# Expert 1's first weights fetched into another tile, three clears of the output moved forward, and the first-layer copies put in another order, in a fused attention and mixture-of-experts kernel

## The chip, the cores and the metric

The kernel runs on one NeuronCore of a Trainium2 chip. The metric is the device time of one execution in microseconds (us). Three runs of the kernel before took 678.64, 680.66 and 685.27 us; the median is 680.66 us. One more execution was profiled; it took 679.25 us, of which 677.5 us lie between the first and the last instruction.

The engines are named as the profile names them: PE (TensorE, matrix multiply), PEld (its weight loads), DVE (VectorE), ACT (ScalarE), POOL (GpSimd) and SP (SyncE, which here only issues transfers). Each engine works through its own instructions in the order in which they were written. SP and POOL each issue transfers in that order too, so a transfer whose source isn't ready holds back every later transfer of the same issuer.

## The reference, cut to what matters

An attention layer over 4 batches, 8 heads, 768 positions and head size 64 feeds a mixture of 8 experts.

```
scores_l = q k^T / 8          kept where |i - j| < 16, else -1e9
scores_s = q kmax^T / 8 + log(32)   kmax: maximum of k over each block of 32
a   = softmax over [scores_l, scores_s]
x   = a [v ; mean of v over each block]          -> 3072 tokens x 512
noisy = x w_gate + log(1 + exp(x w_noise)) * noise
top2, weights = two largest of 8 per token, softmax over the two
out = 0
for e in 8 experts:
    h = relu(x[tokens of e] @ w1[e])      512 -> 1024
    out[tokens of e] += weight * (h @ w2[e])   1024 -> 512
```

All values are float32. The kernel writes every float32 factor of the two expert products as a float16 high part plus a float16 low part and multiplies high by high, high by low and low by high.

## The kernel before, in words

**Attention.** 24 tiles `t` of 128 tokens (128 rows of one batch) run through a software pipeline: in round `t` of the loop at L1087 the scores of tile `t + 2`, the transposes of the probabilities of tile `t + 1`, the product with v of tile `t` and the transpose of the finished x of tile `t - 1` are issued. `norm(t)` (L335) divides by the softmax sum and leaves `X[t]`. `norm_hi` and `norm_lo` (L347 to L358) split it into the high and the low half of `XR[t]`, a tile name with three buffers, so tile `t + 3` takes the buffer of tile `t`; `x_out` (L360) writes it to the DRAM table `xd`. What doesn't belong to the pipeline (the gate in batches of four tiles, loads of weights, transfers) is put at a place `at(time, function)` (L991), where the whole part is the round and the fraction the place in it; `run` issues it there. `.9` is close to the end of a round, ahead of the `x_out(t - 2)` that ends it. After the loop a written-out tail (L1141 to L1221) finishes the last tiles, the gate and the first half of expert 0's first layer; in it DVE carries the gate's small operations one after another.

**Gathers.** Each expert has 816 slots in seven chunks `c`, six of 128 and one of 48. `x_gather(e, c)` (POOL) fetches the x rows of the tokens of a chunk into one of four tiles `XG` (or, for expert 1's first three chunks, `PREV`), `x_trans(e, c)` (SP, a transposing transfer) turns them into `XTE[e]`; expert 0's last three chunks are transposed on PE instead (`x_trans_pe`, L770). Results are added to `out` in DRAM by a gather of the old rows, a DVE operation `y_out` (L954), and a scatter. So `out` must be zero first: `clear(zero, n)` (L996) writes n x 128 rows of zeros from a zeroed tile, 768 KB for n = 3. All eight clears are issued by SP in the tail, after `x_out(23)`.

**Weights.** `w_load(e, i)` (L617) brings one 512 KB block into one of four buffers of the tile `stg`: blocks 0 to 3 are w1 (128 rows each), 4 to 7 are w2. Before a buffer is loaded again, the operations that read it must be over. `w_hi` and `w_lo` make the halves for w2.

**First layer, expert 0** (`mm1`): twelve matmuls for each of the eight column blocks f of w1. **First layer, experts 1 to 7** (`mm1_all`, L836): Winograd's form of the 2 x 2 block product, with seven products instead of eight. It needs sums of blocks of w1 (`w1_sums` on DVE, L653, from blocks k and k + 2; `w1_hi` on ACT, L672; `w1_lo` on DVE, L676; the results for the sums lie in `sh` and `sl`, one pair for even and one for odd experts) and sums of quarters of x (`t_all`, `t_two`, `t_four` on DVE, or `t_diff` on POOL with `t_join` on DVE; `t_hi` on ACT, `t_lo` on DVE; L690 to L724). For each f of four, products 1 to 7 come in the order of `ROUNDS` (L834), a minus sign meaning the f of the round before; product 3 closes the PSUM tile `DD[f]`, and `after` (L842) issues what follows a product: copies of PSUM to SBUF on ACT (`P1`, `U2`, `U3`), additions on DVE (`A`, `DD`, `C22`), and `h_hi` (ACT) and `h_lo` (DVE), which make the halves of h. Product 4 of f adds into the PSUM tile from which `U3[f]` is copied, so it waits for that copy.

**Second layer** (`mm2_turn`, L969): three passes of eight matmuls for a chunk, then `y_out`. The PSUM tile `pt` has two buffers, so the chunk after next waits for `y_out`.

**Order across experts.** Between products and passes a tick is counted, and a plan (L1251 to L1310) tells what each tick issues: `steps(n, e, ...)` puts steps for expert n into the ticks of expert e. In expert 0, ticks 0 to 2 follow the last passes of chunks 0 to 2, ticks 3 to 10 the eight blocks f of the second half of its first layer, and three ticks each follow the passes of chunks 3 to 6. In the others ticks 0 to 27 follow the 28 products. `d` (L1297) shifts the `t_diff` and `t_join` steps that are issued during expert 1.

Of the kernel before, what the change touches and what calls it, by code (L numbers as in the profile page):

```python
# [8 lines left out]
F32 = mybir.dt.float32  # L9
# [11 lines left out]
P = 128  # L21
# [39 lines left out]
def attn_moe(ctx, tc, qt, kt, vt, wgn, noise, w1, w2, out):  # L61
# [552 lines left out]

    SG = {}

    def w_load(e, i):  # L617
        s = stage.tile([P, SW], F32, name="stg")[:, :1024]
        SG[e, i] = s
        if i < 4:  # L620
            nc.sync.dma_start(s, w1[e, i * P:(i + 1) * P, :])
        else:
            i -= 4
            nc.sync.dma_start(s.rearrange("p (c d) -> p c d", c=2),
                              w2[e, 2 * i * P:2 * (i + 1) * P, :].rearrange("(c p) d -> p c d", p=P))
# [202 lines left out]
    def h_hi(f, c0, c1, c):  # L828
        nc.scalar.activation(HT[0][:, f, c0:c1], c, AF.Relu)  # L829

    def h_lo(f, c0, c1, c):
        nc.vector.scalar_tensor_tensor(HT[1][:, f, c0:c1], c, 0.0, HT[0][:, f, c0:c1], op0=OP.max, op1=OP.subtract)
# [3 lines left out]
    def mm1_all(e, tick):  # L836
        X, DD, A, P1, U2, U3, C22 = {}, {}, {}, {}, {}, {}, {}

        def temp(name, n=1):
            return side_pool[0].tile([P, HC], F32, name=name, bufs=n)  # L840

        def after(f, p):  # L842
            g = f + FC // 2
            if p == 1:
                P1[f] = temp("p1")
                nc.scalar.activation(P1[f], X[f], AF.Copy)  # L846
                if f:
                    h_hi(g - 1, HC, CAP, C22[f - 1])
            elif p == 2:
                nc.vector.tensor_add(A[f], A[f], P1[f])  # L850
                if f:
                    h_lo(g - 1, HC, CAP, C22[f - 1]) if f < 3 else None
                h_hi(f, 0, HC, A[f])
            elif p == 4:
                h_hi(g, 0, HC, X[f])
            elif p == 6:
                U2[f] = temp("u2", 2)
                nc.scalar.activation(U2[f], X[f], AF.Copy)
            elif p == 3:
                nc.vector.tensor_add(DD[f], DD[f], U2[f])  # L860
                h_hi(f, HC, CAP, DD[f])
            elif p == 7:
                U3[f] = temp("u3")
                nc.scalar.activation(U3[f], X[f], AF.Copy)
                C22[f] = temp("c22")
                nc.vector.tensor_add(C22[f], DD[f], U3[f])

        for r, ps in enumerate(ROUNDS):
            for p in ps:
                f = r - (p < 0)  # L870
                p = abs(p)
                if p == 1:
                    X[f] = bank()[:, 0, :HC]
                elif p == 5:
                    DD[f] = bank()[:, 0, :HC]
                elif p == 2:
                    A[f] = accs[0].tile([P, 512], F32, name="a")[:, :HC]
                o = DD[f] if p in (3, 5) else A[f] if p == 2 else X[f]
                product(o, e, f, p, p in (1, 5, 2), p in (4, 3, 2))
                after(f, p)  # L880
                g = FC // 2
                if r < 3:
                    if p == 6:
                        h_lo(f, 0, HC, A[f])
                        if f:
                            h_lo(f - 1 + g, 0, HC, X[f - 1])
                    elif p == 3:
                        pass
                    elif p == 7 and f:
                        h_lo(f - 1, HC, CAP, DD[f - 1])  # L890
                else:
                    if p == 6:
                        h_lo(2 + g, HC, CAP, C22[2])
                        h_lo(2 + g, 0, HC, X[2])
                    elif p == 4 and f == 3:
                        h_lo(2, HC, CAP, DD[2])
                    elif p == 2:
                        h_hi(3 + g, HC, CAP, C22[3])
                        h_lo(3 + g, 0, HC, X[3])
                    elif p == 3 and f == 3:  # L900
                        h_lo(3, 0, HC, A[3])
                        h_lo(3 + g, HC, CAP, C22[3])
                        h_lo(3, HC, CAP, DD[3])
                tick()
# [86 lines left out]
    def at(t, f, *a):  # L991
        todo.setdefault(round(t, 3), []).append((f, a))
# [50 lines left out]
    for i in range(3):  # L1043
        at(4.9 + 2 * i, fill, i)
    at(20.8, last_init)
    for b, (t0, t1) in enumerate(BATCH[:4]):
        u = t1 + 2
        at(u - 0.91, gate_gt, b)
        at(u - 0.91, gate_gc, b)
        at(u + 0.09, gate_gl, b)  # L1050
        at(u + 0.09, gate_gd, b)
        at(u + 0.9, gate_a, b)
        at(u + 1.1, gate_b, b)
        at(u + 1.1, gate_m, b)
        at(u + 1.9, gate_p, b)
        at(u + 2.3, lambda b, t: gate_c(b, PO[t]), b, u + 2)
        at(u + 3.02, lambda b, t: gate_d(b, PO[t]), b, u + 2)
        at(u + 3.1, gate_e, b)
        if b == 3:
            break  # L1060
        at(u + 4.1, gate_v, b)
        z = u + (6 if b < 2 else 4)
        at(z + 0.2, gate_o, b)
        at(z + 0.2, gate_f, b, (0,))
        at(z + 1.03, gate_f, b, (1,))
        at(z + 1.9, lambda b, t: gate_t(b, PO[t]), b, z + 1)
        at(z + 2.02, lambda b, t: gate_u(b, PO[t]), b, z + 1)
# [113 lines left out]
    norm_hi(NT - 1)  # L1181
    norm_lo(NT - 1, nc.vector)
    x_out(NT - 1)
    for i in range(8):
        clear(PREV[2], 3)
    for x in HT:
        nc.gpsimd.memset(x[:, :, CAP:], 0.0)
# [35 lines left out]
    def finish_table():  # L1223
        decode(TB.rearrange("p e c w -> p (e c) w"), 0, NS)
        last_ids()
        for c in range(3, NCH):
            x_gather(0, c)
        for f in range(4, 8):
            w_lo(0, f)
        for c in range(3):  # L1230
            x_gather(1, c)
        w_load(1, 0)
        x_trans(0, 3)
        w_load(1, 2)
        x_trans(1, 0)
        x_trans(1, 1)
        w_load(1, 1)
        x_trans(1, 2)
        w_load(1, 3)

    finish_table()
    mm2_high(0, 0)
# [21 lines left out]
    for k, c in ((0, 3), (1, 4), (1, 5), (2, 6)):  # L1264
        put(0, k, x_gather, 1, c)
        put(0, k, x_trans, 1, c)
    steps(1, 0, (
        (2, w1_hi, 0, 0), (3, w1_sums, 0, 0), (3, w1_sums, 0, 1), (3, w1_hi, 0, 1), (4, w1_lo, 0, 0),
        (5, w1_lo, 0, 1, (0,)), (6, w1_lo, 0, 1, (1,)), (6, w1_sums, 1, 0), (6, w1_hi, 1, 0), (7, w1_sums, 1, 1),
        (7, w1_hi, 1, 1), (8, w1_lo, 1, 0), (9, w1_lo, 1, 1, (0,)), (10, w1_lo, 1, 1, (1,)), (10, t_all, 3),  # L1270
        (11, t_alloc), (11, t_two, 0), (11, t_two, 1), (11, t_hi, 3), (11, t_hi, 2), (13, t_all, 1), (13, t_hi, 1),
        (14, t_lo, 3), (14, t_lo, 2), (16, t_lo, 1), (16, t_four), (16, t_hi, 4), (19, t_lo, 4)))
    for i, k in enumerate((14, 16, 18, 19)):
        put(0, k, w_load, 1, 4 + i)
    M2 = 7 * (FC // 2)
# [10 lines left out]
    for e in range(1, E):  # L1286
# [7 lines left out]
            break  # L1294
        n = e + 1
        put(e, 0, w1_alloc, n, True)
        d = 6 if e == 1 else 0  # L1297
        steps(n, e, (
            (1 + d, t_diff, 3, 0), (4 + d, t_diff, 3, 1), (10 + d, t_join, 3),
            (7 + d, t_diff, 1, 0), (11 + d, t_diff, 1, 1), (17 + d, t_join, 1)))  # L1300
# [149 lines left out]
```

## Time and profile before

| | us |
|---|---|
| three runs | 678.64, 680.66, 685.27 |
| profiled execution, its own time | 679.25 |
| its span, first to last instruction | 677.5 |
| PE busy | 639.6 (94%) |
| DVE busy | 492.7 (73%) |
| ACT busy | 318.6 (47%) |
| POOL busy | 319.3 (47%) |
| granted clock of TensorE | 0.994 |
| bytes moved | 125.64 MB |

The attention takes the first 140 us or so, the tail and expert 0 run until about 222 us, and each of the other seven experts takes a little over 63 us. A row of a timeline tells the start, the duration, the engine, the line, the operation, what it writes and reads, and in square brackets how long its engine was idle before and which instruction ended that. In the windows, the columns are the stretch, its length, the busy time and the number of instructions of each engine, the granted clock, the share of the 16 DMA engines that was busy, and GB/s. Ends of matmuls are modelled: a matmul row reaches a little beyond the place where the next one may start.

### The profile page before, as it was taken

The page shows a single profiled execution, that of the slowest core. Times are in us where ns is not written, and L with a number is a line of the kernel's source. Part 1 is how long each engine was busy: PE and PEld are TensorE (multiplying, and loading weights), DVE is VectorE, ACT ScalarE, POOL GpSimd, SP SyncE. Part 2 cuts the span into 40 slices and gives each one's busy share as a digit, 9 for nine tenths or more (in the row PEclk, how much of TensorE's full clock was granted, in tenths as well). Part 3 has the DMA queues.
Part 4 walks back from the last instruction along what each step waited for, and adds up shares of the span by engine and source line. Part 5 has one row for each costly group of instructions (what it writes and reads, how often), then busy time and mean ns, then how long its engine had stood idle before and what let it go on. Part 6 is the DMA issues. An engine that isn't in the chain of part 4 may idle for free.

```text
span 677.5 us, 14084 instructions
## 1 busy us (share of the span) xinstructions
PE 639.6 (94%) x5408; PEld 368.5 (54%) x5408; DVE 492.7 (73%) x905; ACT 318.6 (47%) x679; POOL 319.3 (47%) x459
## 2 busy tenths in 40 slices
PE   7999889989999999999999999999999999999992
PEld 6777667755444654555455445544654555455442
DVE  5748798999479788677958795788688687946410
ACT  2879788852251554156325523542463156326100
POOL 3454344430833656562856276545556551640141
PEclk9999999999999999999999999999999999999997
DMA  8999999769995956727554564567266622431120
GB/s 285 290 294 301 296 313 296 244 159 369 262 189 128 262 178 169 231 88 206 149 183 151 163 192 160 181 156 242 94 167 165 225 84 89 169 109 32 33 84 31
DMA packets 99241, 125.64 MB, mean 185 GB/s; under 512 B 57929, under 2 KB 62801, under 8 KB 99164
## 3 DMA queue, kind: packets, MB, share of 16 engines
q1 hardware_dynamic: 87020, 88.37, 45.8%
q0 software_dynamic: 12144, 36.28, 17.2%
q8 instruction: 44, 0.72, 0.5%
q14 instruction: 33, 0.27, 0.1%
HBM read 87.57 MB, written 26.21 MB: 168 GB/s over the span
## 4 chain that ended last, share of the span: by engine, by line
PE 70%; DVE 11%; ACT 7%; DMA 6%; issue 3%; POOL 1%; SPq 0%; POOLq 0%; DVEq 0%; ACTq 0%
PE pt L939 34%; PE h L824 21%; PE a L824 4%; PE pt L936 3%; DMA stg<-in_w_dram 2%; ACT p L310 2%; DMA hth<-in_vt_dram 1%; DMA q<-in_qt_dram 1%; PE h L788 1%; PE s L296 1%; PE pt L316 1%; DVE rh L541 1%; DVE t L649 1%; ACT pts L319 1%; ACT w2h L629 1%
## 5 line engine op out<-in xcount | busy, mean ns | idle before, releaser
L92 POOL DMA_INDIRECT out_dram<-y,tb x48 | 64.7, 1347 | 165.6 <-DVE y L962 152.3
L939 PEld LDWEIGHTS <-hth 128*128 128x128 f16 x768 | 74.7, 98 | 91.7 <-ACT hth L798 2.5
L939 PE MATMUL pt<-w2h,hth 128*128 128x512 f16 x376 | 89.0, 379 | 2.2 <-ACT hth L798 1.4
L92 POOL DMA_INDIRECT xg<-xd,tb x53 | 68.0, 1282 | 46.2 <-DVE oc L567 24.8
L939 PE MATMUL pt<-w2h,htl 128*128 128x512 f16 x376 | 89.0, 379 | 0.6 <-DVE htl L799 0.6
L939 PE MATMUL pt<-w2l,hth 128*128 128x512 f16 x376 | 88.8, 379 | 0.0
L824 PE MATMUL h<-tx,sh 128*128 128x408 f16 x336 | 78.7, 336 | 0.0
L962 DVE SCALAR_TENSOR_TENSOR y<-pt,tb,prev 128x512 f32<-128x512 f32 x42 | 31.5, 749 | 53.9 <-PE pt L939 53.9
L646 DVE SCALAR_TENSOR_TENSOR w2l<-stg,w2h 128x1024 f16<-128x1024 f32 x32 | 48.5, 1524 | 28.0 <-ACT w2h L629 28.0
L824 PEld LDWEIGHTS <-w1h 128*128 128x128 f16 x448 | 43.2, 98 | 36.6 <-issue 4.7
L939 PEld LDWEIGHTS <-htl 128*128 128x128 f16 x384 | 37.6, 98 | 46.3 <-DVE htl L799 1.1
L693 POOL TENSOR_TENSOR t<-xte 128x816 f32<-128x816 f16 x24 | 41.5, 1755 | 34.5 <-DVE t L649 29.9
L824 PE MATMUL h<-xte,w1h 128*128 128x408 f16 x224 | 57.0, 336 | 0.0
L92 POOL DMA_INDIRECT prev<-out_dram,tb x42 | 50.9, 1212 | 12.7 <-issue 12.7
L358 POOL TENSOR_TENSOR xr<-x,xr 128x512 f16<-128x512 f32 x22 | 25.4, 1156 | 62.8 <-PE pt L316 28.8
L310 ACT ACTIVATE p<-s,nm 128x118 f32<-128x118 f32 x192 | 53.4, 377 | 0.8
L721 ACT ACTIVATE tx<-t 128x816 f16<-128x816 f32 x28 | 24.0, 879 | 55.0 <-DVE t L649 55.0
L846 ACT ACTIVATE p<-h 128x408 f32<-128x408 f32 x28 | 14.3, 512 | 69.2 <-PE h L824 68.9
L824 PEld LDWEIGHTS <-sh 128*128 128x128 f16 x336 | 32.9, 98 | 25.2 <-issue 0.2
L829 ACT ACTIVATE hth<-h 128x408 f16<-128x408 f32 x56 | 27.7, 508 | 36.2 <-DVE h L860 35.0
L824 PE MATMUL h<-tx,sl 128*128 128x408 f16 x168 | 42.7, 336 | 0.0
L674 ACT ACTIVATE sh<-ws 128x1536 f16<-128x1536 f32 x14 | 20.8, 1483 | 41.0 <-DVE ws L649 33.0
(205 smaller groups left out, 1239.1 us busy)
## 6 DMA issues: line engine op xcount, KB each, us to landing
stg<-in_w_dram SPq DMA_DIRECT2D x64, 512.0 KB
hth<-in_vt_dram SPq DMA_DIRECT2D x8, 780.0 KB
vw<-in_vt_dram SPq DMA_DIRECT2D x32, 195.0 KB
q<-in_qt_dram SPq DMA_DIRECT2D x24, 256.0 KB
xd<-xr SPq DMA_DIRECT2D x24, 256.0 KB
out_dram<-prev SPq DMA_DIRECT2D x8, 768.0 KB
kb<-in_kt_dram SPq DMA_DIRECT2D x6, 768.0 KB
htl<-in_vt_dram SPq DMA_DIRECT2D x16, 195.0 KB
```

Source lines behind the costliest of these rows:

```text
L92: return nc.gpsimd.indirect_dma_start(**kw)
L310: nc.scalar.activation(PE_[t][:, a, hp, :], SC[t][:, a, hp, :], AF.Exp, bias=NM[t][:, 1, a, hp:hp + 1], scale=0.125)
L358: engine.tensor_tensor(XR[t][:, DM:], X[t], XR[t][:, 0:DM], op=OP.subtract)
L646: nc.vector.scalar_tensor_tensor(lo, SG[e, i], sc, hi, op0=OP.mult, op1=OP.subtract)
L674: nc.scalar.activation(h, x, AF.Copy, scale=W1S)
L693: nc.gpsimd.tensor_tensor(tt(e, 0 if low else j), xb(e, *i, low), xb(e, *o, low), op=OP.subtract)
L721: nc.scalar.activation(TX[e][:, 0, j - 1], t_of(e, j), AF.Copy)
L824: nc.tensor.matmul(o, lhs[a][:, c], rhs[b][:, c], start=start and n == 0, stop=stop and n == 5, skip_group_check=True)
L829: nc.scalar.activation(HT[0][:, f, c0:c1], c, AF.Relu)
L936: nc.tensor.matmul(py[64 * r:64 * r + 64, :HD], hx[:, f, c * P:c * P + 64], w[:, f, HD * r:HD * r + HD], start=first, stop=final, skip_gro ...
L939: nc.tensor.matmul(py, hx[:, f, c * P:c * P + P], w[:, f, :], start=first, stop=final, skip_group_check=True)
L962: nc.vector.scalar_tensor_tensor(y, py[:, :d], gw, pv[:, :d], op0=OP.mult, op1=OP.add)
```

## The change

Four edits stand in the diff.

- **Loads.** `w_load` can take another home than `stg`: a tile under the name `sh0` or `sl0`, which later holds the sums of expert 2's weights and has the room for a block. Blocks 0 and 2 of expert 1's w1 go there and are issued right after `x_out(23)`. Blocks 1 and 3 take the two earlier places in `finish_table`. The steps that work on expert 1's w1 move up by about two ticks, and `t_lo` of one quarter by one tick.
- **Clears.** Three of the eight clears are put into the attention, at 21.9, 22.8 and 22.9, with `XG[3]` (zeroed at the start) as their source; five stay after the two loads.
- **First-layer order.** For f = 0, 1 and 2, `h_hi(f)` of `DD[f]` isn't issued behind the DVE addition that follows product 3, but behind the copy `U3` of the next f (f = 0, 1), or behind product 4 of f = 3 (f = 2).
- **Sums of x.** `d` is 7 instead of 6: the `t_diff` and `t_join` steps during expert 1 come one tick later.

```diff
-    def w_load(e, i):
-        s = stage.tile([P, SW], F32, name="stg")[:, :1024]
+    def w_load(e, i, home=None):
+        if home:
+            s = late[0].tile([P, 3 * HF], F32, name=home)[:, :1024]
+        else:
+            s = stage.tile([P, SW], F32, name="stg")[:, :1024]
...
             elif p == 3:
                 nc.vector.tensor_add(DD[f], DD[f], U2[f])
-                h_hi(f, HC, CAP, DD[f])
+                if f == FC // 2 - 1:
+                    h_hi(f, HC, CAP, DD[f])
             elif p == 7:
                 U3[f] = temp("u3")
                 nc.scalar.activation(U3[f], X[f], AF.Copy)
+                if 0 < f < FC // 2 - 1:
+                    h_hi(f - 1, HC, CAP, DD[f - 1])
                 C22[f] = temp("c22")
...
                     elif p == 4 and f == 3:
+                        h_hi(2, HC, CAP, DD[2])
                         h_lo(2, HC, CAP, DD[2])
...
     at(20.8, last_init)
+    for t in (21.9, 22.8, 22.9):
+        at(t, lambda: clear(XG[3].bitcast(F32), 3))
...
     x_out(NT - 1)
-    for i in range(8):
+    w_load(1, 0, "sh0")
+    w_load(1, 2, "sl0")
+    for i in range(5):
         clear(PREV[2], 3)
...
         for c in range(3):
             x_gather(1, c)
-        w_load(1, 0)
+        w_load(1, 1)
         x_trans(0, 3)
-        w_load(1, 2)
-        x_trans(1, 0)
-        x_trans(1, 1)
-        w_load(1, 1)
-        x_trans(1, 2)
         w_load(1, 3)
+        for c in range(3):
+            x_trans(1, c)
...
     steps(1, 0, (
-        (2, w1_hi, 0, 0), (3, w1_sums, 0, 0), (3, w1_sums, 0, 1), (3, w1_hi, 0, 1), (4, w1_lo, 0, 0),
-        (5, w1_lo, 0, 1, (0,)), (6, w1_lo, 0, 1, (1,)), (6, w1_sums, 1, 0), (6, w1_hi, 1, 0), (7, w1_sums, 1, 1),
-        (7, w1_hi, 1, 1), (8, w1_lo, 1, 0), (9, w1_lo, 1, 1, (0,)), (10, w1_lo, 1, 1, (1,)), (10, t_all, 3),
-        (11, t_alloc), (11, t_two, 0), (11, t_two, 1), (11, t_hi, 3), (11, t_hi, 2), (13, t_all, 1), (13, t_hi, 1),
-        (14, t_lo, 3), (14, t_lo, 2), (16, t_lo, 1), (16, t_four), (16, t_hi, 4), (19, t_lo, 4)))
+        (0, w1_sums, 0, 0), (1, w1_sums, 0, 1), (2, w1_hi, 0, 0), (2, w1_hi, 0, 1), (2, w1_lo, 0, 0),
+        (3, w1_lo, 0, 1, (0,)), (4, w1_lo, 0, 1, (1,)), (4, w1_sums, 1, 0), (4, w1_hi, 1, 0), (5, w1_sums, 1, 1),
+        (6, w1_lo, 1, 0), (6, w1_hi, 1, 1), (7, w1_lo, 1, 1, (0,)), (8, w1_lo, 1, 1, (1,)), (10, t_all, 3),
+        (11, t_alloc), (11, t_two, 0), (11, t_hi, 3), (11, t_two, 1), (11, t_hi, 2), (13, t_all, 1), (13, t_hi, 1),
+        (13, t_lo, 3), (14, t_lo, 2), (16, t_lo, 1), (16, t_four), (16, t_hi, 4), (19, t_lo, 4)))
...
-        d = 6 if e == 1 else 0
+        d = 7 if e == 1 else 0
```

## The prediction

> **What bounds the kernel now.** I read the page first, then the windows of ten us, then the chain of work that ended last, and then the timelines of the engines where PE has gaps. From the page, and from the windows:
>
> ```profile
> span 677.5 us, 14084 instructions
> PE 639.6 (94%) x5408; PEld 368.5 (54%) x5408; DVE 492.7 (73%) x905; ACT 318.6 (47%) x679; POOL 319.3 (47%) x459
> ...
> 150.00:160.00 10.00, 8.02 (x61) 5.05 (x60) 9.76 (x29) 4.89 (x8) 0.00 (x0) 1.00 0.87 318
> 200.00:210.00 10.00, 8.01 (x37) 3.19 (x36) 8.17 (x11) 3.26 (x5) 4.12 (x6) 1.00 0.86 192
> 210.00:220.00 10.00, 9.06 (x49) 4.24 (x49) 9.83 (x12) 2.65 (x3) 5.14 (x7) 1.00 0.25 71
> ```
>
> PE is the bound, busy 94% of the span. Only its gaps can be won, and the windows tell two kinds: around 150 DVE is full (9.76 of 10) and PE waits for it; around 200 to 220 PE loses some 3 us again. The chain of waits names what lies behind the second, and gives the pace of the later experts:
>
> ```profile
> 142.99 2.56 DMA xd<-xr
> ...
> 185.03 12.27 DMA stg<-in_w_dram
> ...
> 222.29 1.14 PE h L824 x6
> ...
> 252.56 31.08 PE pt L939 x144
> 283.64 2.74 PE pt L936 x48
> 286.38 1.14 PE h L824 x6
> ...
> 293.73 6.21 PE h L824 x36
> ...
> 315.74 31.08 PE pt L939 x144
> ...
> 631.74 31.08 PE pt L939 x144
> ```
>
> In these rows (start, duration, what) a second layer takes 31.08 us for six chunks, 5.18 each, and 2.74 for the last. Thirty-six matmuls, six products, take 6.21, so a product takes 1.035; the first of an expert is 1.14. Twenty-eight products without a stall would be 1.14 + 27 x 1.035 = 29.08. Expert 1 takes 252.56 - 222.29 = 30.27, so it loses 1.19. Expert 2 takes 315.74 - 286.38 = 29.36 and loses 0.28. From 315.74 to 631.74 lie five experts at 63.20, less 33.82 for their second layers: 29.38, so experts 3 to 7 lose 0.28 to 0.30 as well.
>
> **Part one: expert 1's first weights.** The PE rows at the passage from expert 0 to 1, then the rows of DVE, ACT and SP that stand behind them:
>
> ```profile
> 200.34 0.81 PE L939 MATMUL pt<-w2h,hth 128*128 128x512 f16 x3
> 202.55 1.25 PE L939 MATMUL pt<-w2h,hth 128*128 128x512 f16 x5 [1.40 <-ACT hth L798]
> ...
> 213.98 1.89 PE L939 MATMUL pt<-w2h,hth 128*128 128x512 f16 x8 [0.78 <-DVE y L960]
> ```
>
> ```profile
> 179.81 0.75 DVE L960 TENSOR_SCALAR y<-pt,tb 128x512 f32<-128x512 f32 x1 [1.42 <-PE pt L939]
> ...
> 208.08 1.00 DVE L649 SCALAR_TENSOR_TENSOR t<-xte 128x816 f32<-128x816 f16 x1
> ...
> 213.18 0.75 DVE L960 TENSOR_SCALAR y<-pt,tb 128x512 f32<-128x512 f32 x1
> ```
>
> ```profile
> 197.33 1.06 ACT L674 ACTIVATE w1h<-stg 128x1024 f16<-128x1024 f32 x1 [4.50 <-DMA stg<-in_w_dram]
> ```
>
> ```profile
> 169.60 0.36 SPq L621 DMA_DIRECT2D stg<-in_w_dram  x1
> ...
> 173.32 0.51 SPq L621 DMA_DIRECT2D stg<-in_w_dram  x1
> ...
> 185.03 1.56 SPq L621 DMA_DIRECT2D stg<-in_w_dram  x1
> ```
>
> Chunk 3 starts at 200.34. Three chunks and the last one need 3 x 5.18 + 2.74 = 18.28, yet expert 1 starts at 222.29, 21.95 later. So 3.67 are lost, of which I count 3.6 (the chain begins a step a little later than the row does). It is a chain of lateness: the fourth w1 block is issued at 185.03 and lands 12.27 later, ACT has been idle 4.50 for it, `hth` comes late behind it on ACT (1.40), and DVE, which does the last w1 pieces until 208.08, then `t_all`, gets to `y` of chunk 3 only at 213.18, while PE waits for that PSUM buffer (0.78); two smaller gaps have the same origin.
>
> With the change blocks 0 and 2 need no `stg` buffer and are issued near 151; blocks 1 and 3 go out at 169.60 and 173.32. Even with the 12.27 of the slowest row the last lands by 185.6. It is wanted at tick 4, behind the second block f of the first layer, near 190: 4 us of cover. One window more, from 182 to 208 (the third busy time is DVE's):
>
> ```profile
> 182.00:208.00 26.00, 23.43 (x129) 11.76 (x128) 18.13 (x25) 11.11 (x17) 10.22 (x18) 1.00 1.01 205
> ```
>
> DVE had 18.13 us of work there and nearly 8 idle. The first sums move ahead of it: two ticks of two operations of 512 columns, 1.25 us a tick at the 1.00 that 816 columns take at 208.08, and DVE is idle for 1.42 before the `y` at 179.81. So about 15.6 remain from 182 on, without the wait, and DVE could be through near 198. It is then held by PE's own end of the first layer (200.34), with one ACT and one DVE operation behind it (0.5 to 0.6 each, as the rows of L829 and L860 below): `t_all` starts near 201.7 instead of at 208.08, 6.4 earlier. `y` of chunk 3 moves from 213.18 to 206.8; PE wants its buffer at 200.34 + 2 x 5.18 = 210.7. That is 3.9 of cover, and all four gaps go: **-3.6**. What is late next is nothing of DVE, but PE itself. The `t_lo` that moves a tick keeps its place behind `y` on DVE, and swapping `t_hi` with `t_two` crosses two engines: no cost, as both queues keep their order. The tile for the blocks belongs to expert 2's sums, which are first written in tick 33 of expert 1, in its second layer (after 252.56), some 50 us after the last reader. With two blocks fewer in `stg`, expert 1's first w2 blocks find a free buffer without waiting for w1.
>
> **Part two: the order in the first layer.** PE's row in expert 1 with DVE's; then ACT's two rows in expert 2:
>
> ```profile
> 244.12 0.51 PE L824 MATMUL h<-tx,w1h 128*128 128x408 f16 x2 [1.03 <-ACT u L864]
> ```
>
> ```profile
> 241.62 1.00 DVE L649 SCALAR_TENSOR_TENSOR t<-t,t 128x816 f32<-128x816 f32 x1
> 242.54 0.58 DVE L860 TENSOR_TENSOR h<-h,u 128x408 f32<-128x408 f32 x1
> ```
>
> ```profile
> 306.33 0.51 ACT L829 ACTIVATE hth<-h 128x408 f16<-128x408 f32 x1 [1.79 <-DVE h L860]
> 306.74 0.51 ACT L864 ACTIVATE u<-h 128x408 f32<-128x408 f32 x1
> ```
>
> PE waits for `U3` (L864). `U3` waits on ACT behind `h_hi` (L829), that for the DVE addition L860, and that, in expert 1, stands behind a `t_join` of 1.00 (L649). In experts 2 to 7 it stands behind a w2 operation. With `h_hi` behind `U3`, the copy starts when its product ends: ACT was idle 1.79 before. So ACT's 0.41 between the two starts and all of DVE's delay leave the path. Product 7 of f = 2 is the nineteenth and ends at 286.38 + 1.14 + 18 x 1.035 = 306.15, so `U3` is out near 306.75, and PE wants it one product after 306.15, at 307.19: cover 0.4. For expert 1 the later `t_join` (d = 7) cures the same stall a second time. `t_diff` on POOL comes a tick later, 1.035, with its `t_join` a tick later too, so POOL keeps its distance; no `y` scatter is behind it. `h_hi(2)` goes behind product 4 of f = 3 and swaps with `h_hi(7)`; both are done at the same time as before, and `h_lo(2)` about 0.8 later, ahead of the sum for `A[3]`, which the second layer reads as its seventh matmul, 1.3 after its start: cover 0.5, at a cost of zero to 0.3 per expert if it is gone. Sum: expert 1 **-1.2**, the six others 6 x 0.28 = **-1.7**.
>
> **Part three: the clears.** The end of the attention on SP, what follows on ACT, DVE and PE, and three windows of 2 us:
>
> ```profile
> 137.38 0.52 SPq L361 DMA_DIRECT2D xd<-xr  x1
> ...
> 142.99 8.02 SPq L361 DMA_DIRECT2D xd<-xr  x4
> 151.11 9.18 SPq L999 DMA_DIRECT2D out_dram<-prev  x8
> ```
>
> ```profile
> 149.32 0.61 ACT L351 ACTIVATE xr<-x 128x512 f16<-128x512 f32 x1
> ```
>
> ```profile
> 149.97 0.69 DVE L358 TENSOR_TENSOR xr<-x,xr 128x512 f16<-128x512 f32 x1 [0.16 <-ACT xr L351]
> ```
>
> ```profile
> 145.04 0.81 PE L788 MATMUL h<-xte,w1h 128*128 128x384 f16 x4
> ...
> 158.60 0.45 PE L551 MATMUL o<-rh,lh 128*128 128x168 f16 x4 [0.32 <-DVE rh L541]
> ```
>
> ```profile
> 142.00:144.00 2.00, 1.28 (x16) 0.66 (x18) 1.92 (x17) 1.31 (x4) 1.18 (x5) 1.00 0.82 135
> ...
> 148.00:150.00 2.00, 2.00 (x16) 1.23 (x15) 1.74 (x18) 0.79 (x3) 0.00 (x0) 1.00 0.04 9
> ...
> 152.00:154.00 2.00, 1.18 (x12) 0.97 (x12) 1.90 (x12) 0.96 (x2) 0.00 (x0) 1.00 1.00 378
> ```
>
> The first clear comes ahead of `x_out(19)` (137.38) and two transposes, the other two ahead of `x_out(20)` (142.99). Clears alone ran at 378 GB/s, so one of 0.786 MB takes 2.1 us and two take 4.2. `x_out(20)` took 2.56 to land; behind two clears it lands at 142.99 + 2.56 + 4.2 = 149.75. Its `XR` buffer is written next by `norm_hi(23)`, on ACT at 149.32: 0.43 late. Queued behind that are `norm_lo(23)` on DVE at 149.97, the full DVE stream after it, and PE, which waits for DVE at 158.60; so the delay reaches the end. The first clear delays the transposes that the matmuls read at 145.04; SP issued the last of them just ahead of its row at 142.99, so there is little to spare, and it can come a few tenths late, which the gate's transpose on PE, behind four of those matmuls, hands to DVE. I take 0.4 for that, between none and the 2.1 of a whole clear. The Trainium skill (DMA: Bandwidth & Descriptors, Queues, rings and completion order) speaks against so little: each DMA engine takes turns between the queues packet by packet and keeps the order within one. By that rule the first clear halves the rate of POOL's gather for the third transpose, which then is issued later as well, and the total would be near -5.1 instead of -5.7; no row of the kernel before sets a clear against a gather. **Sum +0.8**, from the 0.43 and the 0.4. Ends: 0 or a shade below if the clears slip into the idle engines (share 0.04 at 148 to 150), and +7.9 if they crawl at the 135 GB/s of 142 to 144. I take a value near the lower end because most of their time lies between 145 and 149, next to the row with the idle engines.
>
> What the clears free later is worth nothing: 8 x 0.786 MB end near 168, five and two blocks end near 164.5, and PE has no gap from 165 to 182.
>
> Total: -3.6 - 1.2 - 1.7 + 0.8 = **-5.7**. The profiled execution's own time is 679.25 (its span 677.5 and 1.75 around it), so it would be 673.55. The median of the three runs lies 1.41 above that execution and the lowest 0.61 below; I allow half a us for it and say **674.0**.
>
> **The rivals.** *The passage keeps part of its wait* (0.15). DVE still does `t_all` and two more ahead of `y` of chunk 3; if the transposes of expert 1's x land at 206 rather than before 201, `t_all` starts 2 earlier, not 6.4, and the 0.78 and the gap after it stay in part. Against it: two loads, 1 MB or 2.8 us at 378 GB/s, leave the stretch in which those transposes run. Price 2 us: 676.
>
> *The order edit does nothing* (0.1): `U3` is held by ACT's own w2 copy, or `h_lo(2)` by its new place, so the 1.7 and part of expert 1's 1.2 stay. Against it stands the 1.79 of idle ACT. Then 676.5.
>
> *Slower, by the clears* (0.08). At 135 GB/s the two clears, 1.57 MB, take 11.65, `x_out(20)` lands at 157.2 and `norm_hi(23)` is 7.9 late; with the -6.5 of the rest the time is 679.25 + 1.4 + 0.5 = 681. It becomes slower than before from a landing at 155.8 on, so from 153 GB/s down. For it: the rate of the windows in which gathers and transposes run. Against it: PE reads the last of those transposes at 145.04, so they are over when the two clears begin.
>
> **How the numbers follow.** The forecast has 0.62, the rivals 0.15, 0.1 and 0.08; 0.05 is left for what I don't see. The forecast's own range is 672.2 to 676. Eight in ten: 671.6, a little below the -6.5 without any price, up to 678, which takes in the first two rivals and leaves out the third. About 1% is what a measurement of this kernel can tell from no change: 673.85 and 687.5 against the median. Somewhat less than half of the forecast's chance lies below 673.85 (0.3), with what comes out better than my terms 0.37 together; slower by over 1% needs the third rival and more: 0.04; within 1%: 0.59.
>
> **What would show it.** Right: no wait row of ACT for `stg` between 185 and 200 and PE's start of expert 1 18.3 to 18.4 after the start of chunk 3; each first layer 29.1 in the chain, expert 1's too; `norm_hi(23)` under 1 us later, counted from the start. Wrong: a gap ahead of L939 released by `y`; L864 still behind L829; PE's waits around 152 to 159 longer by more than 1 us; or a clear's rate far from 378 GB/s.

## The result, and the profile after

The changed kernel took 677.96 us (median of 22 runs, 674.06 to 686.6). On the same chip the kernel before took 684.97 us (22 runs, 678.64 to 691.36). The ratio is 0.992, with a 95% interval of 0.9895 to 0.9945: faster by 0.55 to 1.05%, about 5.5 us. The ratio is taken over the runs within 1.5% of the fastest of each kernel (16 and 20 runs, with means of 683.2 and 677.7 us), while the medians of all runs differ by 7.0. The forecast of 674.0 against the 680.66 of three runs was a ratio of 0.990. The time itself is 4.0 above the forecast.

The profiled execution of the changed kernel took 678.34 us. Its page has these lines for the span, the engines and the chain:

```profile
span 676.6 us, 14081 instructions
PE 641.2 (95%) x5408; PEld 372.1 (55%) x5408; DVE 490.7 (73%) x905; ACT 319.3 (47%) x679; POOL 321.7 (48%) x459
...
PE 81%; DVE 6%; DMA 5%; ACT 4%; issue 1%; SPq 1%; POOL 0%; POOLq 0%; DVEq 0%; ACTq 0%
```

PE is still the bound, and the chain runs on it for 81% of the span. The span is only 0.9 shorter than in the profile before, though. The chain of waits of the changed kernel (start, duration, what) shows that the later part did all that was forecast. L946 and L943 are the second layer here (L939 and L936 before), and L827 is the first layer (L824 before):

```profile
206.40 15.54 PE pt L946 x72
221.94 2.74 PE pt L943 x48
224.69 1.14 PE h L827 x6
...
253.77 31.08 PE pt L946 x144
284.85 2.74 PE pt L943 x48
287.59 1.14 PE h L827 x6
...
316.68 31.08 PE pt L946 x144
```

Chunk 3 of expert 0 starts at 206.40 and expert 1 at 224.69, which is 18.29 for the passage. The 21.95 of before was counted from the row of PE, which starts a little ahead of the chain's; counted like that it is 224.69 - 206.24 = 18.45. No load stands in between. Expert 1's first layer takes 253.77 - 224.69 = 29.08 (30.27 before), and expert 2's takes 316.68 - 287.59 = 29.09 (29.36 before).

But chunk 3 started at 200.34 before. So 5.9 us were lost ahead of 206.24, at the end of the attention and in the tail. First come two rows of PE in the kernel before (L384 is the gate's product, L551 a part of the position sums):

```profile
133.65 1.08 PE L384 MATMUL pt<-xt,wg 128*32 128x128 f32 x32 [0.55 <-ACT pts L319]
...
152.82 0.74 PE L551 MATMUL o<-rh,lh 128*128 128x168 f16 x8 [1.29 <-DVE pos L476]
```

These are the rows of SP, ACT and PE in the timeline of the changed kernel (L1006 is a clear, L769 a transpose, L361 `x_out`), and one row of its chain of waits:

```profile
141.04 4.83 SPq L769 DMA_TRANSPOSE xte<-xg  x2
145.92 1.87 SPq L1006 DMA_DIRECT2D out_dram<-xg  x2
147.90 4.11 SPq L361 DMA_DIRECT2D xd<-xr  x3
```

```profile
147.90 6.35 DMA xd<-xr
```

```profile
154.32 0.63 ACT L351 ACTIVATE xr<-x 128x512 f16<-128x512 f32 x1 [0.91 <-DMA xd<-xr]
```

```profile
135.48 1.08 PE L384 MATMUL pt<-xt,wg 128*32 128x128 f32 x32 [0.54 <-ACT pts L319]
...
147.91 1.06 PE L384 MATMUL pt<-xt,wg 128*32 128x128 f32 x26 [0.34 <-ACT xt L372]
...
157.84 0.74 PE L551 MATMUL o<-rh,lh 128*128 128x168 f16 x8 [2.31 <-DVE pos L476]
```

`norm_hi(23)` waits on ACT for `x_out(20)`, which was issued at 147.90 and held the `XR` buffer until about 154.25, 6.35 later. Behind it DVE is late, and PE waits 2.31 at L551, where it waited 1.29 before.

Not all of the 5.9 is the clears'. The gate's batch starts at 135.48 instead of 133.65 in the profile before, which is 1.8 later and ahead of any clear. From there to 147.91 it takes 12.4 instead of 10.3. In that stretch PE waits 2.09 at 141.50 (L366), which the profile before doesn't have, but a wait of 1.93 to 2.03 stands at the same place in four profiles below of kernels without an early clear. The windows of the changed kernel show why that part can't be charged to the clears alone (the column before the last two is the granted clock):

```profile
16.40:19.80 3.40, 3.40 (x72) 2.88 (x64) 1.01 (x4) 1.34 (x6) 0.00 (x0) 0.50 1.07 273
112.00:115.40 3.40, 3.40 (x34) 2.64 (x36) 1.14 (x1) 1.94 (x6) 1.81 (x4) 0.50 0.73 203
142.70:146.10 3.40, 3.40 (x54) 3.09 (x50) 1.72 (x6) 0.58 (x2) 2.74 (x6) 0.50 1.12 334
148.00:152.00 4.00, 3.92 (x49) 2.54 (x50) 3.84 (x19) 1.06 (x4) 0.00 (x0) 1.00 1.10 389
```

In three stretches of 3.4 us PE had half its clock, two of them long before any clear. The profile of the kernel before has none between its first 8 us and PE's last matmul (mean clock 0.994 against 0.986 here). So two single profiles are a poor measure of what the clears cost, and the experiments have to tell.

### The profile page after: what moved, and what is told of

Same layout as the page of the kernel before. It is cut to its first block, busy times and chain, and to the rows that moved or that the text cites. A ratio compares the mean times of both kernels' runs of the same rounds, so it can differ in the third digit from the quotient of the medians.

```text
span 676.6 us, 14081 instructions
## 1 busy us (share of the span) xinstructions
PE 641.2 (95%) x5408; PEld 372.1 (55%) x5408; DVE 490.7 (73%) x905; ACT 319.3 (47%) x679; POOL 321.7 (48%) x459
## 4 chain that ended last, share of the span: by engine, by line
PE 81%; DVE 6%; DMA 5%; ACT 4%; issue 1%; SPq 1%; POOL 0%; POOLq 0%; DVEq 0%; ACTq 0%
PE pt L946 36%; PE h L827 26%; PE a L827 4%; PE h L791 3%; PE pt L943 3%; ACT p L310 2%; PE pt L316 2%; PE s L296 1%; DMA hth<-in_vt_dram 1%; DMA q<-in_qt_dram 1%; PE o L329 1%; DVE rh L541 1%; PE pt L241 1%; ACT pts L319 1%; DVE nm L303 1%
## 5 line engine op out<-in xcount | busy, mean ns | idle before, releaser
L946 PEld LDWEIGHTS <-hth 128*128 128x128 f16 x768 | 74.9, 98 | 89.1
L946 PE MATMUL pt<-w2h,hth 128*128 128x512 f16 x376 | 88.8, 379 | 0.0
L946 PE MATMUL pt<-w2h,htl 128*128 128x512 f16 x376 | 88.8, 379 | 0.0
L946 PE MATMUL pt<-w2l,hth 128*128 128x512 f16 x376 | 88.8, 379 | 0.0
L827 PE MATMUL h<-tx,sh 128*128 128x408 f16 x336 | 78.7, 336 | 0.0
L946 PEld LDWEIGHTS <-htl 128*128 128x128 f16 x384 | 37.6, 98 | 45.3
L827 PEld LDWEIGHTS <-w1h 128*128 128x128 f16 x448 | 43.3, 98 | 33.8 <-issue 1.4
L827 PE MATMUL h<-xte,w1h 128*128 128x408 f16 x224 | 57.0, 336 | 0.0
L827 PEld LDWEIGHTS <-sh 128*128 128x128 f16 x336 | 32.9, 98 | 25.2 <-issue 0.2
L827 PE MATMUL h<-tx,sl 128*128 128x408 f16 x168 | 42.7, 336 | 0.0
L835 DVE SCALAR_TENSOR_TENSOR htl<-h,hth 128x408 f16<-128x408 f32 x56 | 32.2, 574 | 8.4 <-ACT hth L832 8.4
```

The costliest lines, as they stand in the source:

```text
L827: nc.tensor.matmul(o, lhs[a][:, c], rhs[b][:, c], start=start and n == 0, stop=stop and n == 5, skip_group_check=True)
L946: nc.tensor.matmul(py, hx[:, f, c * P:c * P + P], w[:, f, :], start=first, stop=final, skip_group_check=True)
```

## The experiments

The theory was that the loads and the order are worth what was forecast and that the clears cost more than 0.8, through the `XR` buffer. The rivals were that the order or the loads fell short, or that the clears cost by another way. Each ratio below is to the kernel before, run on the same chip. The order, the loads and the clears by themselves and the first run without early clears shared one chip, where the kernel before had a median of 680.57 us; the changed kernel once more, the second run without early clears, the other buffer and the clears after `x_out(22)` shared another (683.86); the last four kernels a third (686.63).

**The order alone.** The kernel before with the moved `h_hi` and `d = 7`:

```diff
-                h_hi(f, HC, CAP, DD[f])
+                if f == FC // 2 - 1:
+                    h_hi(f, HC, CAP, DD[f])
...
-        d = 6 if e == 1 else 0
+        d = 7 if e == 1 else 0
```

> The kernel before with the first-layer order and d = 7 alone; the loads and the eight clears stay where they were. Theory (the terms add): the stall of expert 1 (1.2) and the 0.28 of each of experts 2 to 7 go, so -2.9 us against the kernel before, ratio 0.9957; each first layer takes 29.1 in the chain of waits, and the passage from expert 0 to 1 keeps its 3.6. Rival (the order does nothing, the 6.5 came from somewhere else): 0, with PE still waiting for the copy U3 in every expert.

It took 678.48 us, a ratio of 0.9958 [0.993, 0.9986]: -2.9, as forecast (1.2 + 1.7).

**The loads alone.** The kernel before with the two early blocks and the moved steps; all eight clears stand behind the loads:

```diff
+    w_load(1, 0, "sh0")
+    w_load(1, 2, "sl0")
     for i in range(8):
         clear(PREV[2], 3)
```

> The kernel before with the two early loads, the new places of the other two and the earlier steps, and with all eight clears behind the two loads. Theory: the passage (start of chunk 3 to start of expert 1) falls from 21.9 to 18.3, -3.6 us, ratio 0.9947; the first layers keep their stalls. Rival (the clears had to move for it): two loads ahead of eight clears end the clears 2.8 us later, near 171 instead of 168, the gathers that start at 167.5 come late, and 1 to 3 us of the 3.6 are lost before 200.

It took 676.63 us, 0.9942 [0.992, 0.9965]: -3.9 where -3.6 was forecast. The passage took 18.4 us by the row of PE, and the chain of this kernel then shows the old loss of expert 1 untouched:

```profile
221.76 1.14 PE h L827 x6
...
252.03 31.08 PE pt L942 x144
```

252.03 - 221.76 = 30.27, exactly as before. Loads and order are two separate gains.

**The clears alone.** The kernel before with three early clears and five late ones:

```diff
+    for t in (21.9, 22.8, 22.9):
+        at(t, lambda: clear(XG[3].bitcast(F32), 3))
...
-    for i in range(8):
+    for i in range(5):
```

> The kernel before with only three of the eight clears moved into the attention. First theory (on record): +0.8 us, ratio 1.001, norm_hi of the last tile 0.4 late. Rival one, after the profile of the changed kernel: +3 to +4 us, ratio 1.005, x_out of tile 20 lands 6 us after its issue and the last norm_hi waits for it on ACT. Rival two: no price, since what the profile of the changed kernel lost there is a stretch of half clock and not the transfers: 0.

It took 685.31 us, 1.0059 [1.0032, 1.0087]: +4.0, not +0.8. SP, ACT and PE in its timeline:

```profile
138.55 4.72 SPq L766 DMA_TRANSPOSE xte<-xg  x2
143.32 1.10 SPq L999 DMA_DIRECT2D out_dram<-xg  x2
144.53 3.77 SPq L361 DMA_DIRECT2D xd<-xr  x3
```

```profile
151.60 0.63 ACT L351 ACTIVATE xr<-x 128x512 f16<-128x512 f32 x1 [2.33 <-DMA xd<-xr]
```

```profile
133.05 1.08 PE L384 MATMUL pt<-xt,wg 128*32 128x128 f32 x32 [0.55 <-ACT pts L319]
...
155.11 0.74 PE L551 MATMUL o<-rh,lh 128*128 128x168 f16 x8 [3.55 <-DVE pos L476]
```

The gate's batch starts at 133.05 here. ACT waits 2.33 for `x_out(20)`, and PE's wait at L551 grows from 1.29 to 3.55, by 2.26. The windows of the same kernel show what follows:

```profile
152.00:156.00 4.00, 0.89 (x10) 0.77 (x10) 3.67 (x12) 3.26 (x6) 0.00 (x0) 1.00 0.55 204
156.10:159.50 3.40, 3.40 (x13) 1.64 (x12) 3.30 (x11) 0.18 (x1) 0.00 (x0) 0.51 1.04 377
```

PE is nearly idle from 152 to 156, and then runs at half clock for 3.4 us. At half clock at most 1.7 of these can be lost, so the two together give by an estimate 2.3 to 4.0 us. The mean granted clock over the 12 runs was 0.9876, against 0.9906 over the 29 runs of the kernel before on that chip. That is about one such stretch more per run (3.4/2 in 677 is 0.0025).

**The whole change without the early clears.** The changed kernel with all eight clears behind the two loads, on two chips:

```diff
-    for t in (21.9, 22.8, 22.9):
-        at(t, lambda: clear(XG[3].bitcast(F32), 3))
...
-    for i in range(5):
+    for i in range(8):
```

> The changed kernel without the three early clears: all eight clears stand behind the two loads. First theory: -6.5 us against the kernel before, 0.8 faster than the changed kernel (ratio to before 0.9905). Rival one (early clears cost 3 to 4): 3 to 4 us faster than the changed kernel, ratio 0.987. Rival two (the early clears are needed): as in the rival of the loads alone, the gathers behind eight clears and two loads come late, and it is 1 to 3 us slower than the changed kernel.

> The changed kernel without the early clears once more, beside the changed kernel on one chip. Theory: ratio to before 0.9896 as in its first runs, 3 to 4 us faster than the changed kernel. Rival (the cost of the early clears in the profiles was chance): within 1 us of the changed kernel.

It took 674.28 us, 0.9896 [0.9857, 0.9934], on the first chip (5 runs), and 676.36 us, 0.9885 [0.9841, 0.9928], on the second (6 runs). On the first chip the gain of 6.3 between the medians (7.1 by the ratio) lies near the sum of order and loads (2.1 and 3.9 between the medians, 2.9 and 3.9 by the ratios). In its profile PE's wait at L551 is 1.11. Beside the second run stood the changed kernel itself:

> The changed kernel once more, to stand beside the next three on one chip. Theory now: the first-layer order gives 2.9, the loads 3.9, and the three early clears take back 3.5 to 4 in the stretch from the gate of the fifth batch (the 32 matmuls of L384 near 134) to the second half of expert 0's first layer; this stretch is 53.2 us long with the early clears and 49.2 to 49.8 without. So ratio 0.992 to 0.995.

It took 677.97 us, 0.9891 [0.9845, 0.9937]. Without the early clears it is 1.6 us less by the medians and 0.4 by the ratios. The theory asked for 3 to 4 and the rival for under 1, but the two intervals overlap almost wholly, so a price between zero and some 4 us fits, and these runs don't decide. In this profile the mechanism is there again; ACT, PE and the window after them:

```profile
154.78 0.63 ACT L351 ACTIVATE xr<-x 128x512 f16<-128x512 f32 x1 [2.62 <-DMA xd<-xr]
```

```profile
158.29 1.28 PE L551 MATMUL o<-rh,lh 128*128 128x168 f16 x8 [3.85 <-DVE pos L476]
```

```profile
156.70:163.50 6.80, 5.21 (x21) 3.05 (x21) 6.63 (x22) 1.79 (x5) 0.00 (x0) 0.50 0.90 294
```

PE's wait is 2.56 longer than before, and half clock holds for 6.8 us from its middle on.

**Another buffer for the last `XR`.** The changed kernel, where tile 23 writes its halves into a place of expert 1's w1 tile that is still unused, so `norm_hi(23)` doesn't depend on `x_out(20)`:

```diff
-        XR[t] = work.tile([P, 2 * DM], F16, name="xr", bufs=3)
+        if t == NT - 1:
+            XR[t] = WT[1]["w1l"][:, 0, :]
+        else:
+            XR[t] = work.tile([P, 2 * DM], F16, name="xr", bufs=3)
```

> The changed kernel, but the halves of the last tile's x go into a part of expert 1's w1l tile, free at that time, instead of the XR buffer that x_out of tile 20 has to leave first. Theory (what the clears cost is the wait of the last norm_hi for that buffer): the stretch falls from 53.2 to about 50.3, 2.5 to 3 us faster than the changed kernel, ratio to before 0.988. Rival (the cost is the transposes, gathers and fetches that lie behind the clears in the queues): no more than 1 us faster than the changed kernel, another wait stands in its place.

It took 677.18 us, 0.9897 [0.9854, 0.9941]. The rows of ACT (the tile has the other name now) and of PE (L554 is L551 of the others):

```profile
152.38 0.61 ACT L354 ACTIVATE w1l<-x 128x512 f16<-128x512 f32 x1
```

```profile
155.87 0.74 PE L554 MATMUL o<-rh,lh 128*128 128x168 f16 x8 [1.29 <-DVE pos L479]
```

ACT no longer waits, and PE's wait is back at 1.29, which fits the buffer as the cause of both. The time, however, is only 0.8 below that of the changed kernel beside it, less than these six runs can tell from nothing, and the number is the rival's. The profile tells one reason. `x_out(20)` is issued at 146.73 here, so with a landing of 6.35 to 7.06 later, as in the two profiles of the changed kernel, it lands by an estimate at 153.1 to 153.8. With the shared buffer ACT would then have waited only 0.7 to 1.4 at 152.38. So the buffer is the best-supported cause of PE's gap, but its removal isn't shown to bring back 2.5 to 3 us.

**The three clears after `x_out(22)`.**

```diff
     x_out(NT - 2)
+    for i in range(3):
+        clear(XG[3].bitcast(F32), 3)
```

> The changed kernel with the three clears behind x_out of tile 22 instead of in the attention, so that only x_out of tile 23, the loads and the other clears lie behind them. Theory: the price of the early clears goes, and what they are good for stays (all clears are over before the gathers at about 168); the stretch takes 49.2 to 49.5, ratio to before 0.989 to 0.990, 3 to 4 us faster than the changed kernel and 0.3 to 0.6 faster than the one without early clears. Rival: x_out of tile 23 is now late and the gathers, which read what it wrote, lose 1 us or more.

It took 677.99 us, 0.9919 [0.9884, 0.9955], no better than the changed kernel. The theory of 3 to 4 us isn't borne out. The wait at L551 is 1.29, so `XR` is free in time. But its profile has another loss, ahead of the second half of expert 0's first layer. PE's row there in this kernel:

```profile
187.93 1.60 PE L791 MATMUL h<-xte,w1h 128*128 128x432 f16 x4 [4.48 <-ACT xte L778]
```

The same row had a wait of 0.58 before (at 182.82), and has 1.46 in the first profile of the changed kernel and 2.83 in the second. PE's small transposes end and ACT's copies of them start late, behind nothing that the profile names. The wait is 4.79 in the kernel with two late clears below, and 1.05 and 1.09 in two kernels without an early clear, so it isn't the clears' alone. The two waits over 4 us have 6.8 us of half clock with them (from 186.2 here, and from 188.2 with two late clears). What makes them stays open.

**One clear, and two.** The kernel before with the first early clear only (seven stay in the tail), and with the other two only (six stay). Set against the loop of the changed kernel, the two edits are:

```diff
-    for t in (21.9, 22.8, 22.9):
+    for t in (21.9,):
```

```diff
-    for t in (21.9, 22.8, 22.9):
+    for t in (22.8, 22.9,):
```

> The kernel before with the first of the three early clears alone (at 21.9, ahead of x_out(19) and two transposes; seven clears stay in the tail). Theory A, the cost of the three clears lies in the two behind the transposes, which stand ahead of x_out(20): then this one costs 0.4 to 1 us (ratio 1.001), the matmuls of the first layer's half read their transposes at most 1 us later counted from the gate batch's L384, and norm_hi(23) keeps its 15.7 us behind L384 to within 1 us. Theory B, the first clear carries most of it, because the gather and the transposes for chunk 2 run beside it and DVE's gate chain waits behind PE: then +2 to +4 us (1.003 to 1.006), and the stretch from L384 to the second half of the first layer grows from 49.2 to about 52.

> The kernel before with the two later early clears alone (at 22.8 and 22.9, between the transposes and x_out(20); six clears stay in the tail). Theory A expects +2.5 to +4 us (1.004 to 1.006), x_out(20) landing some 5 us after its issue and norm_hi(23) 18 us or more behind L384. Theory B expects under 1 us (1.001), with norm_hi(23) under 1 us later and the stretch from L384 to the second half of the first layer at 49.2 to 50.

They took 683.13 us, 0.9975 [0.9937, 1.0013], and 684.15 us, 0.9976 [0.9933, 1.0018], beside 686.63. Neither shows a cost (the intervals reach up to +0.9 and +1.2 us), and both theories fall: one asked for +2.5 of the two late clears, the other for +2 of the first. PE's row at L551 with the first clear only, then with the two late ones only:

```profile
155.96 0.74 PE L551 MATMUL o<-rh,lh 128*128 128x168 f16 x8 [1.10 <-DVE pos L476]
```

```profile
156.24 0.74 PE L551 MATMUL o<-rh,lh 128*128 128x168 f16 x8 [1.30 <-DVE pos L476]
```

In neither profile does `norm_hi(23)` wait for `x_out(20)`. That wait appears in the three profiles that have all three clears ahead of `x_out(20)` and the shared buffer (0.91, 2.33 and 2.62), and in no other one. Why two clears don't make it isn't shown. With the two late ones `x_out(20)` is issued at 146.62, 12.03 behind the gate's batch (134.59), which is no earlier than the 11.48 (144.53 - 133.05) with the clears alone. But ACT comes to `norm_hi(23)` only at 152.75, 18.16 behind the batch, while with the clears alone it was there 16.2 behind (151.60, less its wait of 2.33). So in this profile ACT was late too, and the buffer was free when it came. Besides, these two kernels stood on another chip than the three clears alone. Whether the three clears cost more than their parts, or cost less on this chip, stays open.

**`h_hi` alone, and `d = 7` alone.** One time and one profile of each, for the first layers:

> The kernel before with h_hi behind the copy U3 alone, d still 6. If the order alone cures the stall at U3, expert 1's first layer takes 29.1 us as with both (before: 30.27), and experts 2 to 7 take 29.1 too (before: 29.38). If the t_join on DVE is what holds expert 1, its first layer keeps 0.5 us or more of the 1.19.

> The kernel before with d = 7 alone. Experts 2 to 7 keep 29.38 us for the first layer. If the prediction is right that d = 7 cures expert 1's stall a second time, expert 1 takes 29.1 to 29.4; if the order is what counts, it keeps 29.7 or more.

They took 678.65 and 681.33 us, beside 686.63. The chain with `h_hi` alone, and then with `d = 7` alone:

```profile
253.46 31.08 PE pt L943 x144
...
287.28 1.14 PE h L824 x6
...
316.37 31.08 PE pt L943 x144
```

```profile
254.56 31.08 PE pt L939 x144
...
288.38 1.14 PE h L824 x6
...
317.73 31.08 PE pt L939 x144
```

Expert 2 takes 29.09 with `h_hi` alone and 29.35 with `d` alone, so the gain of the later experts is the order's, as forecast. Expert 1 starts at 223.26 and 223.24, so it takes 30.2 and 31.3 up to its second layer: in these single profiles neither edit alone cures it. PE's waits in expert 1, with `h_hi` alone and with `d = 7` alone:

```profile
239.43 0.50 PE L824 MATMUL h<-tx,sh 128*128 128x408 f16 x2 [0.46 <-ACT p L846]
...
246.06 0.50 PE L824 MATMUL h<-tx,sh 128*128 128x408 f16 x2 [0.26 <-ACT p L846]
```

```profile
239.51 0.51 PE L824 MATMUL h<-tx,w1h 128*128 128x408 f16 x2 [1.61 <-ACT u L864]
...
246.11 0.51 PE L824 MATMUL h<-tx,w1h 128*128 128x408 f16 x2 [0.23 <-ACT u L864]
```

With the moved `h_hi`, `U3` holds PE nowhere. With `d = 7` alone `U3` holds it as before, and longer. Both profiles have one slow DVE operation just ahead of the first of these waits; DVE's and POOL's rows with `h_hi` alone:

```profile
235.07 2.86 DVE L646 SCALAR_TENSOR_TENSOR w2l<-stg,w2h 128x1024 f16<-128x1024 f32 x1
```

```profile
235.10 1.73 POOL L693 TENSOR_TENSOR t<-xte 128x816 f32<-128x816 f16 x1
```

The w2 piece takes 2.86 instead of 1.23, 1.63 more, while POOL's `t_diff` of 1.73 starts within 0.03 of it. With `d = 7` alone the same piece takes 2.87 at 235.15, and POOL's operation starts at 235.19. The Trainium skill (SBUF — State Buffer, SBUF: two separate sides) says that DVE and GpSimd share a pair of SBUF ports as an exclusive lock: when the DVE operation has two SBUF inputs and the GpSimd operation reads SBUF, the one that starts first has the ports for its whole instruction and the other blocks. The durations agree with DVE blocked by POOL's operation: 1.23 + 1.73 = 2.96, against 2.86. The starts don't show it, since the record has DVE's 0.03 ahead. In the two profiles with both edits (the order alone, and the changed kernel) PE waits nowhere in expert 1's first layer, which took 29.09 and 29.08. That this DVE piece is what delays PE with one edit is argued from the rows and not tested, and whether `d = 7` is needed can't be told from these two profiles.

## Why the prediction was right or wrong

**The passage: right.** 18.29 (18.45 by the row of PE) against a forecast 18.28 to 18.4, no wait of ACT for `stg`, and -3.9 in time against -3.6. The rival that a part of the wait stays is out.

**The first layers: right in the sum.** 29.08 and 29.09 against 29.08, and -2.9 in time (with 1.9 to each side, so that the tenth agrees is luck). The rival that the order does nothing is out. One step isn't borne out: that the later `t_join` "cures the same stall a second time" in expert 1. By itself it cured nothing, and the order by itself left a loss there, in a profile where a DVE operation met one of POOL's.

**The clears: the failed step of the sum.** The term was +0.8, and alone they cost +4.0 [2.2, 5.9]. The path was the right one, the `XR` buffer behind `x_out(20)`, and the mark that was to show a wrong forecast was met: PE's wait at L551 grew by more than 1 us (1.02, 2.26 and 2.56 in three profiles). `norm_hi(23)`, which was to come under 1 us later, came 5.0 later in the first profile of the changed kernel, 1.8 of it ahead of any clear. The rate isn't what failed: all transfers of the window from 148 to 152 moved 389 GB/s, against the 378 assumed. Two things were mis-sized.

First, "behind two clears it lands at 142.99 + 2.56 + 4.2 = 149.75" let `x_out(20)` be issued when it was before. The landing was sized well (6.35, 6.99 and 7.06 from its issue in three profiles, against 6.76). But the issue moved. Counted from the gate's batch it came 142.99 - 133.65 = 9.34 behind before, and 144.53 - 133.05 = 11.48 behind with the clears alone (row L384 at 133.05), so 2.1 later. 0.43 + 2.1 is 2.5 late, and ACT waited 2.33. Of the 2.1, 1.2 (from 143.32 to 144.53) is the time that SP needs to issue two clears, which the sum had at nothing; in the first profile of the changed kernel it is 2.0 (145.92 to 147.90). The other 0.9 isn't shown to be the first clear's. SP was through with the two transposes 10.3 behind the gate's batch here, and in the eight profiles without an early clear 9.3 to 11.1 behind it, so the profile that the forecast was read from lies at the early end. With the first clear alone it was 11.6 (146.68 - 135.10), so half a us by it isn't excluded.

The rule set against the forecast (the Trainium skill, DMA: Bandwidth & Descriptors, Queues, rings and completion order) pointed to the third transpose, and to a total nearer -5.1. No run here shows clearly that the first clear makes a transpose later, and the first clear alone cost nothing measurable. The 0.4 set aside for it is neither shown nor refuted.

Second, nothing in the sum said what a longer wait of PE does to its clock. In both profiles where PE waited 3.55 or 3.85 us here, a stretch of half clock of 3.4 or 6.8 us came with it or right behind; at 2.31 none did. The waits of 4.48 and 4.79 ahead of the first layer's second half had 6.8 us of it each. So a wait that is 2.3 us longer can cost by an estimate up to 1.7 on top, half of 3.4. The Trainium skill (TensorE: Matmul & The Clock Gate, Part 1: The HAM clock gate) tells of a free-running window of 3413 ns, and of half rate after an idle one. The traces agree in the length and in these four waits, but half clock also came behind shorter waits (last section).

**The sum.** By their own runs the parts give -2.9 - 3.9 + 4.0 = -2.8, a ratio of 0.996, and the whole measured 0.992. The three intervals reach 1.9, 1.5 and 1.9 us to each side, together some 3.1, so the two don't contradict each other. The forecast sum of -5.7 lies next to the -5.5 of the whole. If the clears cost 4.0 there as well, that is luck; if not, -5.5 + 6.8 leaves 1.3 for them. The runs leave open how much they cost inside the whole: 1.6 by the medians on the one chip where both stood side by side, where anything between zero and 4 fits. In the two profiles of the whole PE's wait was 1.0 and 2.6 longer, and only the second had the half clock with it, so the price may differ from run to run; that is argued, not shown.

**The level: the failed step of the time.** The 674.0 was worked out from a profile of before that had no stretch of half clock while PE had work, and from a median of three runs. "I allow half a us for it" made 679.75 the time of the kernel before. The median of 22 runs was 684.97, 5.2 more. That is more than the 4.0 by which the time was missed: 684.97 x 0.990 is 678.1. That the missing half clock is what put the profile so low is argued, not shown. Of the chances, "within 1%" was given 0.59 and "faster by over 1%" 0.37; the ratio 0.992 lies within, with an interval that reaches just past 1%. The range's upper end, 678.0, was 0.04 away, so that the time lies inside the range is luck, as the level was 5.2 too low.

## What to carry to other kernels

When transfers are put into a busy queue, count the issuer's own time too, and add it to the landing time: here the issue of two clears alone held the next transfer back by 1.2 to 2.0 us. Read the place of that transfer from more than one profile, since it moved by 1.7 us, counted from the gate's batch, between profiles that had no clear there. All four PE waits of 3.5 us and more in the 14 profiles, the start aside, came with half clock, so look for the gaps that are already long. And price such a change over many runs of the kernel before: a profile without any disturbance lies near the lowest of its runs, not in their middle.

## What the runs showed of the hardware

Between the first 8 us and PE's last matmul, PE's stretches at half clock are 3.4 us or twice that in the eleven profiles that have any, and none is in the other three. They go with much of the spread between runs. Over the 22 runs of the changed kernel the time went from 674.06 us at a mean clock of 0.993 to 686.6 us at 0.982. A straight line through time and clock of the runs on the three other chips, with a level of its own for each kernel, gives 1.4 to 2.0 us for each 0.0025 of clock. At equal clock, by the same line, the clears alone cost 2.4 us and not 4.0 (to within 1.3), so half clock isn't all of their price. Some stretches came behind gaps of only about 2 us: in the changed kernel the one at 142.7 follows a wait of 2.09 at 141.50, where the kernel with `d = 7` alone has a wait of 2.03 at 140.22 and full clock behind it.

```profile
141.50 0.63 PE L366 MATMUL pt<-ident,x 128*128 128x128 f32 x4 [2.09 <-DVE wa L518]
```

```profile
140.22 0.63 PE L366 MATMUL pt<-ident,x 128*128 128x128 f32 x4 [2.03 <-DVE wa L518]
```
